# Two MLPs behind an attention block: stages run one by one over all tokens, with a seven-product form in halves of 384 tokens

## The chip, the cores and the metric

The kernel runs on one core of a Trainium2 chip. The metric is the device time of one execution in microseconds (us). Its instructions go to five engines: TensorE (PE, matmuls, with weight loads shown apart as PEld), VectorE (DVE), ScalarE (ACT), GpSimd (POOL) and SyncE (SP, which issues most DMAs).

## The reference

```python
# attention over q, k, v of shape (4, 8, 576, 64), causal, plus a memory term M_prev, z_prev
x = (g * mem_out + (1 - g) * local)            # 2304 tokens x 512
# first MLP, 1536 hidden columns
h = silu(x @ moe_w_gate) * (x @ moe_w_val)     # 2304 x 1536
y = h @ moe_w_out                              # 2304 x 512
# second MLP, 2048 hidden columns
u = y @ moe2_w_in
a = where(u >= 1, u, where(u <= -1, 0, (u + 1)**2 / 4))
out = a @ moe2_w_out                           # 2304 x 512
```

## The kernel before

All matrix products of the MLPs are done with each operand cut in a high and a low part (`PARTS`, line 1067): three matmuls, low by high, high by low and high by high, make one product. A unit `f` is 128 hidden columns, 12 of them in the first MLP and 16 in the second. The MLP weights come in an encoded form and are decoded on chip (`Weights.number`, lines 873 to 941: on DVE two masks, a clamp, a shift, a multiplication and an addition; then `split` makes the two parts).

Two plans are made one after the other by the class `Plan` (line 112), a list scheduler: each task has an engine, a cost, a priority, dependencies and buffers, and the simulated order is the order in which each engine gets its instructions. The engines themselves then run in that order and wait on semaphores.

The first plan is attention, 16 pairs of heads (`Attention.pair`, line 412), four for each batch entry of 576 tokens. Scores, maxima, exponentials, a scaling on POOL (line 735), transposes on PE (lines 769, 786 and 746), copies of these, and the product with the values (`av`, lines 811 and 818). Each pair's result is stored to `xs` in DRAM (line 847). Three groups of 512 tokens (`GROUPS`, line 58) also get their gate and value products for the first six units in this plan (`early_unit`, line 1107, operand tile `xh`, matmuls of line 1074): 432 matmuls of 512 columns, 144 for each group, whose results are stored in DRAM (`gv`).

The second plan is both MLPs. Tokens go in five blocks (`BLOCKS`, line 51: four of 512, one of 256). Block by block: gate and value products (`up_matmuls`, line 1070, operand `xb`), SiLU and product (`hidden`, line 1251), the products with `moe_w_out` (`down`, line 1408), which accumulate over the 12 units in four PSUM banks, and then `pieces` (line 1431), which makes from one block of y the seven operands of a Winograd form of Strassen's scheme and stores them (`ys`). The second MLP runs in three phases of units (`PHASES`), and in each over all blocks: `hidden2` (line 1356) does seven products of 256 columns where the plain form has eight, `hidden1` (line 1337) the plain form for the small block; `down2` (line 1596) adds up the output, and partial sums go to DRAM and back between phases. In `hidden2` the copies c1 (line 1394), c5 and c2 (line 1382) on ACT and the sums v1 and v2 (line 1389) on DVE stand between the products, and PE fills these gaps with queued `down2` products (`fill`, line 1332).

Of the kernel before, what the change touches and what calls it, by code (L numbers as in the profile page):

```python
# [11 lines left out]
U32 = mybir.dt.uint32  # L12
# [16 lines left out]
D1 = 8  # L29
UNITS1 = 12  # L30
# [3 lines left out]
NOACT = 4  # L34
WARM = 8
AHEAD = 30
# [3 lines left out]
OWN = 2  # L40
XB, OP, RAW, HP, TP, WA = 12, 5, 3, 3, 3, 5
SU = 2
UNITS, HALVES = 20, 5
PHASES = (2, 3, 3)
OVER, KEPT = 4, 1

GROUP_AT, X_AT = (-58356.8242, -57686.563, -55609.5288), (21938.2824, -38157.4904, 79878.1715)

FIRST = (0, 8, 1, 2, 9, 3, 4, 10, 5, 6, 11, 7)
BLOCK = 512  # L50
BLOCKS = ((0, 512), (512, 512), (1024, 512), (1792, 512), (1536, 256))
LAST = (8, 9, 10, 11, 0, 1, 2, 3, 4, 5, 6, 7)
ORDERS = ((3, 4, 0, 1, 2), (2, 4, 0, 3, 1), (1, 0, 2, 3, 4))
STAYS = 2
HB = BLOCK // 2
HS = S // 2

GROUPS = (512, 1024, 1536, 1920, 2304)
HT = 512
MASKED = -8.0e9  # L60
# [51 lines left out]
class Plan:  # L112
# [7 lines left out]
    def __init__(self, start=None, over=None, lat=None, slow=None, stay=0, turn=0):  # L120

        self.slow, self.stay, self.turn = slow or {}, stay, turn
        self.over, self.late = over, {**self.LAT, **(lat or {})}
        self.tasks, self.caps, self.taken, self.start = [], {}, {}, start or {}
# [10 lines left out]
    def add(self, eng, dur, prio, fn, deps=(), uses=(), lat=0, behind=None, port=False, form=0):  # L135
# [3 lines left out]
             "lat": lat + self.late[eng], "next": [], "follow": [], "wait": 0, "n": len(self.tasks)}  # L139
# [11 lines left out]
    def dma(self, prio, times, fn, deps=(), uses=(), behind=None):  # L151
# [3 lines left out]
        return self.add("DMA", sum(times), prio, lambda: None, [t], uses)  # L155

    def order(self):
# [29 lines left out]
        while len(out) < len(self.tasks):  # L187
            for eng, heap in ready.items():
                if busy[eng]:
                    continue  # L190
                skipped, found, best = [], None, None
                while heap:
# [9 lines left out]
                    if all(len(free[k]) >= v for k, v in need.items()):  # L202
# [3 lines left out]
                        best = best or t  # L206
                    skipped.append(e)
# [643 lines left out]

class Weights:
# [3 lines left out]
    def __init__(self, ctx, tc, units, dram):  # L856
        self.tc, self.nc, self.first = tc, tc.nc, units
        self.dram = dram
        self.pools = [ctx.enter_context(tc.tile_pool(name="w1", bufs=1))]

    def unit(self, place):
        return self.pools[place.slot >= self.first].tile([P, 2, 512], F32R, name="wu", tag=f"wu{place.slot}")

    def half(self, place):
        return self.pools[1].tile([P, 2, 256], F32R, name="wh", tag=f"wh{place.slot}")

    def begin(self, ctx, plan, bufs, name, reuse):
        pool = lambda tag, n: ctx.enter_context(self.tc.tile_pool(name=f"{tag}_{name}", bufs=n, reuse_waits=reuse))
        self.p = {tag: pool(tag, 1 if tag == "wA" else n) for tag, n in bufs.items()}
# [3 lines left out]
    def number(self, plan, src, prio, s, i_F, places, act=True, behind=None):  # L873
# [3 lines left out]
        i_raw, i_S = plan.inst("raw"), plan.inst("wS")  # L877
        words = lambda x: x.rearrange("p (n t) -> p n t", t=2)

        def load():  # L880
            s["raw"] = self.p["raw"].tile([P, 1024], U32, name="raw", tag="raw")
# [61 lines left out]
    def split(self, plan, prio, t, src, dst, n, uses, act=True):  # L943
# [8 lines left out]
                     t, uses)  # L952
# [3 lines left out]
    def parked(self, plan, tag, prio, t, old, tile, shape):  # L956


        store = plan.dma(prio, [364 * shape[-1] // 128], lambda: self.nc.sync.dma_start(home, f32(tile())), [t], [old])
        home = self.dram.tile(shape, F32, name=f"park{store['n']}")  # L960
        return store, home

    def fetched(self, plan, tag, prio, store, home, put, behind):
        new = plan.inst(tag)
        t = plan.dma(prio, [364 * home.shape[-1] // 128], lambda: self.nc.sync.dma_start(f32(put(new)), home), [store], [new],
                     behind=behind)
        return new, t

    def decode(self, plan, tag, src, prio, act=True, behind=None, park=False):
        i_F, i_w = plan.inst("wA"), plan.inst(tag)  # L970
        s = {"i": i_w}

        def dst():
            if "w" not in s:
                s["w"] = self.unit(i_w)
            return s["w"]

        t = self.number(plan, src, prio, s, i_F, [i_w], act, behind)
        s["t"] = self.split(plan, prio, [t], lambda: f32(s["F"]), dst, 512, [i_F, i_w], act)
        if park:  # L980
            s["park"] = [self.parked(plan, tag, prio, s["t"], i_w, dst, (P, 2, 512))]
        return s

    def back(self, plan, s, tags, prio, behind):


        t = []
        for j, ((store, home), tag) in enumerate(zip(s["park"], tags)):
            def put(place, j=j):
                w = self.half(place) if j == 3 else self.unit(place)  # L990
                if "at" in s:
                    s["w"][j] = w
                else:
                    s["w"] = w
                return w

            i, x = self.fetched(plan, tag, prio, store, home, put, behind)
            behind = plan.last
            t.append(x)
            if "at" in s:  # L1000
                s["i"][j] = i
            else:
                s["i"] = i
        s["t"] = t if "at" in s else t[0]
        s["load"] = behind

    def pair(self, plan, tag, half, srcs, prio, behind=None, park=False):
# [5 lines left out]
        places = [plan.inst(tag) for _ in range(3)] + [plan.inst(half)]  # L1013
# [3 lines left out]
        def dst(j):  # L1017
            if j not in w:
                w[j] = self.half(places[3]) if j == 3 else self.unit(places[j])
            return w[j]  # L1020

        t = [self.number(plan, srcs[0], prio, s[0], i_F[0], [*places, *i_F, *i_C], behind=behind)]
        t.append(self.number(plan, srcs[1], prio, s[1], i_F[1], [], behind=s[0]["load"]))
        lo, up = slice(0, 256), slice(256, 512)
# [13 lines left out]
        for fn, deps, uses in combos:  # L1038
            made.append(plan.add("DVE", e_dve2(256), prio, fn, deps + made[-1:], uses))
        ends = [self.split(plan, prio, [t[0]], lambda: F(0, slice(0, 512)), lambda: dst(0), 512, [i_F[0], places[0]])]  # L1040
        for j in (1, 2):
            ends.append(self.split(plan, prio, [made[-1]], lambda j=j: C(j, slice(0, 512)), lambda j=j: dst(j), 512,
                                   [places[j], i_C[j - 1]]))
        ends.append(self.split(plan, prio, [t[1]], lambda: F(1, up), lambda: dst(3), 256, [i_F[1], places[3]]))

        at_ = ((0, 0), (0, 256), (2, 256), (3, 0), (1, 0), (1, 256), (2, 0))
        park = [self.parked(plan, tag, prio, t, places[j], lambda j=j: dst(j), (P, 2, 256 if j == 3 else 512))
                for j, t in enumerate(ends)] if park else None
# [620 lines left out]
```

## Time and profile before

| | |
|---|---|
| median of 3 runs | 1046.08 us (1045.47 to 1047.13) |
| span of the profiled execution, first to last instruction | 1043.8 us |
| own time of the profiled execution | not given; the median of the runs is 2.3 us above its span |
| PE busy | 1029.0 us (99%) |
| mean granted TensorE clock | 0.998 of 2.4 GHz |

The span is what the profile divides; the time of a run is read here as the span and the 2.3 us that lie around it. PE's busy time is that of pipelined matmuls, so the length of a chain of matmuls is read from the starts of its first and of the next one.

### The profile page before, as it was taken

How to read it: one execution, taken by the hardware profiler on the slowest of the kernel's cores; microseconds unless marked ns; L12 is line 12 of the kernel's file. 1: busy time of each engine (PE TensorE's matmuls, PEld its weight loads, DVE VectorE, ACT ScalarE, POOL GpSimd, SP SyncE). 2: the span in 40 equal slices, each digit the busy share in tenths (PEclk: the TensorE clock that was granted, in tenths of full speed). 3: DMA queues.
4: the chain of work that ended last, by engine and by line, in shares of the span. 5: the costliest groups of instructions: out<-in, count | busy, mean ns of one | idle time of the engine just before them, and what ended most of it. 6: DMA issues, size and time to landing. Idle time of an engine off the chain costs nothing.

```text
span 1043.8 us, 17548 instructions
## 1 busy us (share of the span) xinstructions
PE 1029.0 (99%) x6096; PEld 867.2 (83%) x6096; DVE 674.1 (65%) x1515; ACT 564.6 (54%) x1314; POOL 215.8 (21%) x301
## 2 busy tenths in 40 slices
PE   6999999999999999999999999999999999999998
PEld 5667777778788898888888889999899999899997
DVE  4888888870145688868687767844575767643343
ACT  5987898863222355535353435645564555544443
POOL 7899989992000000000000000000000000000000
PEclk9999999999999999999999999999999999999999
DMA  7776663342785799757777797999689878865422
GB/s 179 190 206 186 177 174 115 99 146 105 248 291 192 251 355 362 239 194 253 271 269 281 257 317 262 356 415 401 214 310 334 307 265 279 273 227 184 161 82 82
DMA packets 172074, 248.12 MB, mean 238 GB/s; under 512 B 72913, under 2 KB 99537, under 8 KB 171985
## 3 DMA queue, kind: packets, MB, share of 16 engines
q1 hardware_dynamic: 170078, 245.64, 69.1%
q10 hardware_dynamic: 1906, 1.35, 0.4%
q8 instruction: 49, 0.80, 0.3%
q14 instruction: 41, 0.33, 0.1%
HBM read 165.15 MB, written 81.79 MB: 237 GB/s over the span
## 4 chain that ended last, share of the span: by engine, by line
PE 96%; POOL 1%; DVE 1%; DMA 1%; ACT 0%; issue 0%; SPq 0%; DVEq 0%; POOLq 0%
PE mm L1074 29%; PE acc L1602 19%; PE mm L1323 18%; PE acc L1418 14%; PE av L818 4%; PE s L646 3%; PE t L769 2%; PE av L811 2%; PE s L680 2%; PE t L786 1%; POOL a L735 1%; PE tq L542 1%; PE tk L531 1%; PE tp L600 1%; PE t L746 1%; DMA kn<-in_q_dram 0%
## 5 line engine op out<-in xcount | busy, mean ns | idle before, releaser
L1602 PE MATMUL acc<-wu,h 128*128 128x512 f32 x864 | 210.3, 391 | 0.0
L1074 PE MATMUL mm<-xb,wu 128*128 128x512 f32 (+1 forms) x1008 | 201.0, 359 | 0.0
L1074 PEld LDWEIGHTS mm<-xb,wu 128*128 128x128 f32 x1008 | 170.0, 189 | 28.3
L1602 PEld LDWEIGHTS acc<-wu,h 128*128 128x128 f32 x864 | 157.4, 188 | 29.3
L1323 PE MATMUL mm<-xb,wu 128*128 128x256 f32 x1188 | 153.9, 283 | 0.0
L1323 PEld LDWEIGHTS mm<-xb,wu 128*128 128x128 f32 x1188 | 150.0, 192 | 3.6 <-ACT mm L1394 0.3
L1418 PE MATMUL acc<-h,wu 128*128 128x512 f32 (+1 forms) x720 | 151.8, 368 | 0.0
L1418 PEld LDWEIGHTS acc<-h,wu 128*128 128x128 f32 x720 | 125.7, 189 | 22.4
L1235 ACT CAST h<-t 128x512 fp32r<-128x512 f32 (+1 forms) x140 | 80.7, 579 | 91.8 <-PE acc L1418 36.4
L1238 DVE TENSOR_TENSOR h<-t,h 128x512 fp32r<-128x512 f32 (+1 forms) x140 | 88.1, 634 | 49.8 <-ACT h L1235 49.1
L1307 ACT ACTIVATE t<-mm,half 128x512 f32<-128x512 f32 (+1 forms) x80 | 51.6, 645 | 116.5 <-PE mm L1323 72.2
L1074 PE MATMUL mm<-xh,wu 128*128 128x512 f32 x432 | 106.6, 401 | 0.0
L1313 DVE SCALAR_TENSOR_TENSOR t<-mm,t 128x512 f32<-128x512 f32 (+1 forms) x80 | 50.8, 635 | 75.0 <-ACT t L1310 74.5
L1122 ACT COPY gvo<-mm 128x512 f32<-128x512 f32 (+1 forms) x80 | 43.2, 543 | 99.9 <-PE mm L1074 90.1
L735 POOL TENSOR_SCALAR a<-a,r,OGP 128x256 f32<-128x256 f32 (+4 forms) x144 | 96.0, 677 | 5.1 <-ACT a L667 3.4
L1074 PEld LDWEIGHTS mm<-xh,wu 128*128 128x128 f32 x432 | 80.0, 188 | 19.1 <-issue 0.9
L667 ACT ACTIVATE a<-a,mn 128x256 f32<-128x256 f32 (+3 forms) x128 | 71.0, 566 | 9.8 <-DVE mn L660 9.6
L890 ACT ACTIVATE wA<-raw 128x512 f32<-128x512 f32 x64 | 43.0, 673 | 34.8 <-DMA raw<-in_moe_w_out_dram 18.4
L449 DVE COPY R<-t 128x512 f32<-128x512 f32 (+1 forms) x48 | 30.0, 640 | 44.9 <-PE t L769 44.8
L660 DVE CUSTOM_DVE_ANT_0 a<-s,mask 128x512 f32<-128x512 f32 (+3 forms) x128 | 55.0, 485 | 5.5 <-PE s L646 5.1
L951 ACT CAST wu<-wA 128x512 fp32r<-128x512 f32 x56 | 34.6, 619 | 30.8 <-DVE wA L920 23.1
L895 DVE TENSOR_SCALAR wA<-wA 128x512 f32<-128x512 f32 x68 | 29.8, 439 | 32.5 <-ACT wA L890 31.3
(133 smaller groups left out, 1413.3 us busy)
## 6 DMA issues: line engine op xcount, KB each, us to landing
xb<-ys SPq DMA_DIRECT2D x69, 512.0 KB, 6.3
park<-wu SPq DMA_DIRECT2D x40, 512.0 KB, 6.6
wu<-park SPq DMA_DIRECT2D x40, 512.0 KB, 8.9
xb<-xs SPq DMA_DIRECT2D x32, 512.0 KB, 7.5
gv<-gv SPq DMA_DIRECT2D x32, 512.0 KB, 9.7
ys<-yo SPq DMA_DIRECT2D x31, 512.0 KB, 5.0
gv<-gvo SPq DMA_DIRECT2D x60, 256.0 KB, 3.8
raw<-in_moe_w_out_dram SPq DMA_DIRECT2D x28, 512.0 KB, 7.1
```

What stands on the lines that cost most here:

```text
L660: nc.vector.tensor_tensor_reduce(a, st[f"s{h}{tag}"][:, at_[c]:at_[c] + kl[c]], self.mask0[:, 512 - kl[c]:512], -0.125, 3.0e38, ALU.add, A ...
L667: nc.scalar.activation(a, a, AF.Exp, bias=mn[:, o:o + 1], scale=-1.0, accum_out=sm[:, o, 0:1])
L735: nc.gpsimd.tensor_scalar(a, a, st["mn"]["r"][:, o:o + 1], self.OGP[:, n, o:o + 1], op0=ALU.mult, op1=ALU.mult)
L1074: nc.tensor.matmul(out, kt_of(unit, pw, kt), x[kt][:, px, cols], start=(kt == 0 and i == 0), stop=(kt == KT - 1 and i == 2))
L1122: nc.scalar.copy(s["o", j], s[j][:, 0:gt])
L1235: nc.scalar.copy(s["h"][:, 0], s["t"])
L1238: nc.vector.tensor_sub(s["h"][:, 1], s["t"], f32(s["h"][:, 0]))
L1307: nc.scalar.activation(mk_t(o), src(), AF.Relu, bias=half, scale=0.5)
L1313: nc.vector.scalar_tensor_tensor(o["t"], src(), 1.0, o["t"], op0=ALU.max, op1=ALU.min)
L1323: nc.tensor.matmul(out, pair["k"](k, pw, j), y["x"][piece][:, px, j], start=first and not (i or j), stop=last and j == 1 and i == 2, skip_ ...
L1418: nc.tensor.matmul(state[m][:, 0:n], l, r, start=(begin and i == 0), stop=(end and i == 2), skip_group_check=True)
L1602: nc.tensor.matmul(state[m], s["h"][:, px, m * P:(m + 1) * P], unit["w"][:, pw], start=(begin and i == 0), stop=(end and i == 2), skip_gro ...
```

## The change

The second plan is written anew, and the first one loses two thirds of its early products.

- Attention: only tokens 0 to 511 keep their early products. For the other two groups the tasks stay in the plan as ghosts, which take their simulated time and buffers but issue nothing. The decoded gate and value weights of the first six units lie in slabs that three units share (`SPOTS`).
- Tokens go in three blocks of 768, each in two halves of HB = 384 tokens, so six groups of 384.
- Gate and value of units 0 to 5 for tokens 512 to 2303 are done in the plain form (`plain`), those of units 6 to 11 in the seven-product form (`chain`), for which the operands are made from x (`x_pieces`). The hidden layer is stored to DRAM (`hs`).
- Then all of `moe_w_out` (`down`), group by group; then all of the second MLP's first product in the seven-product form (`chain`, stored unbounded to `h2s`); then all of its second (`down2`), with the bound taken there. There are no partial sums in DRAM.
- The weights that are used in a later stage are decoded early and parked in DRAM (`parked`). PE's order is fixed by hand; every other task has the latest start that PE's order allows as its priority (`late_starts`).
- The first two pairs of x loads of the second plan are issued on POOL's queue, the next on SP's.

```diff
-BLOCKS = ((0, 512), (512, 512), (1024, 512), (1792, 512), (1536, 256))
-HB = BLOCK // 2
-GROUPS = (512, 1024, 1536, 1920, 2304)
+NK = 3
+NG = 2 * NK
+HB = NT // NG
...
+    def late_starts(self, end):
...
+        for t in reversed(self.tasks):
+            at = t["due"]
+            if at is None:
+                ends = [x["prio"][0] - t["lat"] for x in t["next"]] + [end if t["by"] is None else t["by"]]
+                at = min([min(ends) - t["dur"]] + [x["prio"][0] for x in t["follow"]])
+            t["prio"] = (at, t["n"])
...
             t_x[b] = [at.pair(b, n) for n in range(NP)]
-            for tok in [g for g in groups if (g.stop - 1) // S == b < B - 1]:
+            if b < B - 1:
+                tok, ghost = slice(b * HT, (b + 1) * HT), b > 0
                 stored = [[t_x[e][kt] for e in range(tok.start // S, b + 1)] for kt in range(KT)]
-                xh = load_x(plan, xs, fpool, "xh", tok, X_AT[b], stored)
+                xh, last = early_x(tok, X_AT[b], stored, ghost, last)
                 for f in range(D0):
-                    early_unit(plan, at.ps, f, tok, xh, gpool, GROUP_AT[b], "gvo", bank="bank",
-                               own=b == B - 2 and f >= D0 - OWN)
+                    early_unit(f, xh, GROUP_AT[b], b == B - 2 and f >= D0 - 2, ghost)
...
+    def quarter(kb, r, c, ahead, queue="SP"):
...
+            (nc.gpsimd if queue == "POOL" else nc.sync).dma_start(
+                f32(s["x"]), xs[:, 2 * r:2 * r + 2, :, cols(2 * kb + c)])
...
+    def plain(f, qs, c, span, t_out, kept):
...
+                for kt in range(KT):
+                    for i, (pw, px) in enumerate(PARTS):
+                        nc.tensor.matmul(o[:, 0:n], u["k"](pw, kt), qs[kt // 2, c]["at"](px, kt % 2)[:, span],
+                                         start=(kt == 0 and i == 0), stop=(kt == KT - 1 and i == 2))
...
+    def chain(S, x, kind, ends):
...
+        t1 = prod(0, "a", True, [], [i_e])
+        t5 = prod(4, "d", True, [])
+        c1 = add_act(HB, lambda: nc.scalar.copy(bank(s, "e", i_e)[:, 0:HB], P_("a")), [t1], [i_a, i_e])
+        c5 = add_act(HB, lambda: nc.scalar.copy(s5(), P_("d")), [t5], [i_d, h_s])
+        settle()
+        t6 = prod(5, "a", False, [c1])
+        c2 = add_act(HB, lambda: nc.scalar.copy(u2(), P_("a")), [t6], [i_a, h_u])
+        t2 = prod(1, "e", False, [c1])
+        t3 = prod(2, "d", False, [c5])
+        v1 = add_dve(HB, lambda: nc.vector.tensor_add(u2(), u2(), P_("d")), [c2, t3], [i_d, h_u], by=soon())
+        t7 = prod(6, "a", False, [c2])
+        v2 = add_dve(HB, lambda: nc.vector.tensor_add(s5(), s5(), P_("a")), [t7, c5], [i_a, h_s])
...
+    def down(g):
...
+        for i in range(F1 // 2):
...
+            for m in range(KT):
+                marks.append(pe(e_pe(6, HB), lambda m=m, prod=prod: prod(m), [h["t"]] + [y for u in us for y in u["t"]],
+                                [h["i"], state["i"][m]] + [y for u in us for y in u["i"]]))
...
+    for kb, c, queue, ahead in ((0, 1, "POOL", 0), (1, 0, "POOL", 0), (1, 1, "SP", 0)):
+        for r in range(2):
+            qs[kb][r, c] = quarter(kb, r, c, ahead, queue)
...
+    parks = [wts.parked(plan, out_rows(moe_w_out, f)) for f in range(F1)]
...
+        ends = kept + [plain(f, qs[0], 1, slice(HT - HB, HB), t, []) for f in (2 * i, 2 * i + 1)]
...
+    for i in range(D0 // 2):
+        for kb in (1, 2):
+            for c in range(2):
+                t = flat("h")
+                ends = [plain(f, qs[kb], c, slice(0, HB), t, []) for f in (2 * i, 2 * i + 1)]
...
+    for n, (i, j) in enumerate(todo):
+        for kb in range(NK):
...
+            chain(sets[i, j], xp[kb], ("gate", "val")[j], {"T": silus, "t": None if j == 0 else done, "then": then})
...
+    parks2 = [wts.parked(plan, out_rows(moe2_w_out, f), gate(PARK_AHEAD)) for f in range(F2)]
...
+    for kb in range(NK):
+        yp[kb] = y_pieces(kb)
...
+    for p in range(F2 // 2):
+        for kb in range(NK):
...
+            chain(pairs[p], yp[kb], "up", {"T": T, "then": then})
...
+    for g in range(NG):
+        down2(g)
```

One `prod` of a chain is six matmuls of 384 columns, a chain seven of them. In a chain `settle()` issues t4, the last product of the chain before. A `plain` call is 24 matmuls, a `down` call 144 of 384 columns; `y_pieces` calls `down` for both halves of a block and makes the seven operands of its y; a `down2` call is 144 matmuls of 512 columns.

## Rows read from the trace of the kernel before

**Rows 1.** The page: busy time by engine, and 40 slices of the span.
```profile
PE 1029.0 (99%) x6096; PEld 867.2 (83%) x6096; DVE 674.1 (65%) x1515; ACT 564.6 (54%) x1314; POOL 215.8 (21%) x301
...
PE   6999999999999999999999999999999999999998
...
POOL 7899989992000000000000000000000000000000
```

**Rows 2.** Busy time by stretch, PE's early products (tile xh) alone: stretch, length, busy.
```profile
60.00:234.00 174.00, 38.81 (x144) 1.00 0.54 156
234.00:278.40 44.40, 33.96 (x144) 1.00 0.42 153
278.40:330.00 51.60, 33.86 (x144) 1.00 0.76 252
```

**Rows 3.** Timeline of PE, 234 to 330 us: start, length, instructions.
```profile
234.03 32.31 PE L1074 MATMUL mm<-xh,wu 128*128 128x512 f32 x138
...
270.95 0.76 PE L811 MATMUL av<-P,MZ 128*64 128x320 f32 x4
...
278.45 21.73 PE L1074 MATMUL mm<-xh,wu 128*128 128x512 f32 x92
...
312.15 18.08 PE L1074 MATMUL mm<-xb,wu 128*128 128x512 f32 x79
```

**Rows 4.** Timeline of POOL, its last instructions.
```profile
236.34 1.15 POOL L594 TENSOR_TENSOR p<-p,nrm 128x576 f32<-128x576 f32 x1 [2.96 <-DVE nrm L590]
237.48 5.53 POOL L735 TENSOR_SCALAR a<-a,r,OGP 128x256 f32<-128x256 f32 x9
```

**Rows 5.** Timeline of the end.
```profile
1032.88 6.99 PE L1602 MATMUL acc<-wu,h 128*128 128x512 f32 x30
...
1039.94 1.02 SPq L1587 DMA_DIRECT2D out_dram<-oo  x2
```

**Rows 6.** The chain that ended last, in order of time: start, length, what.
```profile
411.55 5.44 PE acc L1418 x24
...
636.37 5.76 PE mm L1074 x48
```

**Rows 7.** Timeline of PE: the end of a pause near the start.
```profile
18.75 0.66 PE L769 MATMUL t<-ident,a 128*128 128x128 f32 x4 [3.90 <-POOL a L735]
```

**Rows 8.** Stretches of PE behind that pause: length, busy, granted clock.
```profile
20.00:22.00 2.00, 1.37 (x7) 0.50 0.64 141
22.00:24.00 2.00, 2.00 (x11) 0.66 0.74 159
```

**Rows 9.** All engines in a stretch of the MLPs.
```profile
400.00:500.00 100.00, 100.00 (x442) 82.79 (x442) 81.07 (x153) 49.48 (x87) 0.00 (x0) 1.00 0.73 253
```

**Rows 10.** Groups by line and shape: busy us, mean ns | idle before.
```profile
L1323 PEld LDWEIGHTS mm<-xb,wu 128*128 128x128 f32 x1188 | 150.0, 192 | 3.6 <-ACT mm L1394 0.3
L1238 DVE TENSOR_TENSOR h<-t,h 128x512 fp32r<-128x512 f32 x112 | 76.7, 687 | 43.6 <-ACT h L1235 43.2
L901 DVE SCALAR_TENSOR_TENSOR wA<-raw,wA 128x512 uint32<-128x512 uint32 x68 | 48.9, 719 | 0.5
...
L898 DVE TENSOR_SCALAR wA<-wA 128x512 uint32<-128x512 uint32 x68 | 30.6, 450 | 0.7
...
L449 ACT COPY R<-t 128x384 f32<-128x384 f32 x48 | 22.4, 478 | 8.5 <-PE t L786 5.7 <-PE t L769 2.2
...
L1389 DVE TENSOR_TENSOR mm<-u,mm 128x256 f32<-128x256 f32 x32 | 13.7, 428 | 37.7 <-PE mm L1323 37.4 <-ACT yo L1496 0.3
```

**Rows 11.** DMA issues: KB each, median us from issue to landing.
```profile
gv<-gv SPq DMA_DIRECT2D x32, 512.0 KB, 9.7
...
xh<-xs SPq DMA_DIRECT2D x12, 512.0 KB, 6.1
```

More of the change, by code (lines that the diff above doesn't have):

```diff
@@ L27 @@
 D0 = 6
-D1 = 8
-UNITS1 = 12
 FIRST_PAIRS = 3
@@ L982, in decode @@
-        return s
[L984 to L1005, printed above, removed]
@@ L1211, in tile_attention_two_moe @@
-    blocks = [slice(e, e + n) for e, n in BLOCKS]
-    size = lambda tok: tok.stop - tok.start
-    first = [(kind, f) for f in range(D0, D1) for kind in ("gate", "val")]
-    first += [(kind, f) for f in FIRST for kind in ("gate", "val", "wout") if (kind, f) not in ready + first]
-    for i, (kind, f) in enumerate(first):
-        table, w, cut = tables[kind]
-        table[f] = wts.decode(plan, "W", cut(w, f), -20 if i < 2 * (D1 - D0) else 10 * FIRST.index(f) - 10,
-                                act=i >= NOACT)
@@ L1219, in tile_attention_two_moe @@
[L1219 to L1231 removed]
+    plan.cap("X", XS, range(X1))
@@ new lines, in tile_attention_two_moe, with pe @@
+    for tag, n in (("wh", WH), ("T", TP), ("su", SU), ("mm", 8)):
+        plan.cap(tag, n)
+    for n, u in enumerate(first):
+        if n % 3 == 0:
+            held = [Inst("X") for _ in range(2)]
+            for j, i in enumerate(held):
+                i.held, i.slot = True, 2 * (n // 3) + j
+        units[u]["i"] = [held[j] for j in {x[0] for x in SPOTS[n % 3]}]
+        units[u]["t"] = []
+    seq, waiting = [], []
+    clock = [0]
+    def pe(cost, fn, deps, uses):
+        t = plan.add("PE", cost, None, fn, deps, uses, behind=seq[-1:])
+        t["due"] = clock[0]
+        clock[0] += cost
+        seq.append(t)
+        return t
@@ new lines, in gate, with add_act, add_dve, bank @@
+    def gate(ahead, t=None):
+        t = clock[0] if t is None else t
+        past = [x for x in seq[-400:] if x["due"] <= t - ahead]
+        return past[-1:]
+    def add_act(n, fn, deps, uses, **kw):
+        return plan.add("ACT", e_act(n), None, fn, deps, uses, **kw)
+    def add_dve(n, fn, deps, uses, **kw):
+        return plan.add("DVE", e_dve2(n), None, fn, deps, uses, **kw)
+    def bank(s, name, i):
+        if name not in s:
+            s[name] = mm.tile([P, HT], F32, name="mm", tag=f"mm{i.slot}")
+        return s[name]
@@ L1320, in product @@
-    def product(pair, y, k, piece, out, first, last):
-        for j in range(2):
-            for i, (pw, px) in enumerate(PARTS):
-                nc.tensor.matmul(out, pair["k"](k, pw, j), y["x"][piece][:, px, j], start=first and not (i or j),
-                                 stop=last and j == 1 and i == 2, skip_group_check=True)
-    seq, queue = [], []
-    def next_pe(cost, prio, fn, deps, uses):
-        seq.append(plan.add("PE", cost, prio, fn, deps, uses, behind=seq[-1:]))
-        return seq[-1]
@@ L1636, in tile_attention_two_moe, with prod @@
-    fill(len(queue))
+        def prod(k, name, begin, deps, more=()):
+            def f():
+                o = bank(s, name, at_[name])[:, 0:HB]
+                for j in range(2):
+                    for i, (pw, px) in enumerate(PARTS):
+                        nc.tensor.matmul(o, S["k"](k, pw, j), x[k]["at"](px, j), start=begin and not (i or j),
+                                         stop=j == 1 and i == 2, skip_group_check=True)
+            return pe(e_pe(6, HB), f, deps + [S["t"][k], x[k]["t"]], [at_[name], S["i"][k], x[k]["i"], *more])
@@ new lines, in tile_attention_two_moe, with make @@
+    for r in range(2):
+        qs[0][r, 0] = quarter(0, r, 0, 8000)
+    xp = {0: x_pieces(qs[0])}
+    for c in range(2):
+        for r in range(2):
+            qs[2][r, c] = quarter(2, r, c, 8000)
+    sets, kept, wout = {}, {}, []
+    todo = [(i, j) for i in range(D0 // 2, F1 // 2) for j in range(2)]
+    long = 3 * 7 * e_pe(6, HB)
+    start = clock[0] + D0 // 2 * 8 * 2 * e_pe(12, HB)
+    due = {x: start + n * long for n, x in enumerate(todo)}
+    def make(i, j):
+        w = (moe_w_gate, moe_w_val)[j]
+        sets[i, j] = wts.pair(plan, [in_cols(w, f) for f in (2 * i, 2 * i + 1)], gate(SET_AHEAD, due[i, j]), seq[-1:])
```

848 lines of the change are left out of this document (390 added, 458 removed).

## The prediction

> **What bounds the kernel now.** I read the page first: PE is busy for 1029.0 of 1043.8 us, and every slice but the first and the last has 90% or more of it; POOL works in the first ten slices only [rows 1]. So PE's work is the time, but for attention, where POOL could bound as well. Then I asked where PE's early products stand. Of 432 matmuls a third, the first group, runs before 234 us, spread through attention; the other 288 come in two lumps behind it, 144 in 234.0 to 278.4 us and 144 in 278.4 to 330 us [rows 2]. The timeline of PE shows them as two almost unbroken runs, and the MLPs begin at 312.15 us [rows 3]. POOL's last instruction ends at 237.48 + 5.53 = 243.0 us [rows 4]. The reader is to see that attention's other engines are done at 243 us, and that PE owes 288 early products after that point: here PE alone bounds. The MLPs' PE work ends at 1032.88 + 6.99 = 1039.87 us, and 3.9 us of copies and output DMA follow [rows 5]. A matmul of 512 columns takes 5.44/24 = 0.2267 us, one of 256 takes 5.76/48 = 0.120 us [rows 6]; at 2.4 GHz the columns alone are 0.2133 and 0.1067, so each matmul costs its columns and 0.0133 us, whichever its width. One of 384 is then 0.160 + 0.0133 = 0.1733 us; no row has one, and the bounds from the two widths beside it differ by nothing.
>
> **The change, part by part.**
>
> *Early products.* 288 matmuls of 512 columns leave, all of them after 234.03 us: 288 x 0.2267 = 65.3 us. Not all of that is gained, since they cover attention's end. Behind 234.03 us PE has only the last pair's transposes and two `av` blocks, and the transposes wait for POOL's nine scalings, 237.48 to 243.0 us [rows 4], which do not move: what stands ahead of 234 us is the first group, and that stays. The two blocks of `av` take 278.45 - 270.95 = 7.5 us [rows 3]. With about 0.85 us for a hop and the last five transposes (an estimate: four take 0.66 us [rows 7]), PE ends attention at 243.0 + 0.85 + 7.5 = 251.35 us. PE now pauses from 234.0 to about 238 us. Such a pause of 3.90 us near the start [rows 7] was followed by a granted clock of 0.50 and 0.66 in the next two stretches of 2 us [rows 8], which is (0.50 + 0.34) x 2 = 1.7 us of lost work, 1.2 GHz being the lower level. I take it as paid again: 253.0 us. Below, nothing is lost: 251.35.
>
> The Trainium skill's page "TensorE: Matmul & The Clock Gate", section "HAM oscillation — how this bites in real kernels", warns of just this: a pause between bursts of matmuls makes the next burst start at the lower clock. By that rule, the trace agrees (0.50 behind the pause).
>
> *Hand-off.* The first `plain` needs two quarters of x, 768 KB each, issued on POOL's queue, so behind POOL's last scaling at 243.0 us. The trace has no DMA of POOL. The nearest rows are 512 KB in 6.1 us at attention's end and 9.7 us at the slowest [rows 11]. At 6.1 x 1.5 = 9.2 us they land at 252.2, just hidden by `av`; at 9.7 x 1.5 = 14.6 us, and one more for issuing two, at 258.6, which would cost 5.6 us. I take hidden, as the tokens 384 to 767 were stored long before and the DMAs have little else to do there, and keep 258.6 for the range.
>
> *MLPs on PE.* From the code: plain 6 units x 24 = 144 matmuls of 256 columns for tokens 512 to 767, and 4 x 144 = 576 of 384; gate and value chains 18 x 42 = 756; `down` 864; second MLP's chains 24 x 42 = 1008; that is 3204 of 384 columns. `down2` has 864 of 512, as before. Sum: 144 x 0.120 + 3204 x 0.1733 + 864 x 0.2267 = 17.3 + 555.4 + 195.9 = 768.5 us. Before it is 1039.87 - 312.15 = 727.7 us [rows 3, 5], so the MLPs grow by 40.8 us: they take over the 288 products as 144 x 256 and 4 halves, and give back a part by seven products for eight. Counted over everything, it is 47,616 columns and 204 matmuls fewer, 19.8 + 2.7 = 22.6 us of PE.
>
> The same page, section "Back-to-back issue gap", puts a warm matmul at its columns over 2.4 GHz and 2.5 ns. By that the 22.6 us would be 19.8 + 0.5 = 20.4 us; the trace has 13.3 ns [rows 6], so the row is used.
>
> *DVE and ACT under the MLPs.* The tightest stretch is plain and chains together, 17.3 + 99.8 + 131.0 = 248 us of PE. On DVE a decoding is three passes of about 0.70 and three of 0.45 us, 3.45 us [rows 10], and with the low part (0.687) 4.1 us. 12 parked units: 50 us. Six sets of two units, with their sums and splits: 6 x 11.3 = 68 us. A pass over 384 columns lies between 0.428 (256) and 0.687 (512), so 0.557; over 768 it is 0.95. Three blocks of x operands, 12 passes of 0.95 each: 34 us. 18 chains with v1 and v2 and nine with four multiplications: 40 us; the plain products' multiplications: 21 us. Together 213 us, 86%. That is near what DVE had in 400 to 500 us, 81 of 100 us with PE at 100 [rows 9], so it stays cover, not bound. ACT has less. The stores and loads of `hs` and `h2s` replace the `ys`, `gv` and partial-sum traffic, and a group's hidden layer is stored two chains, 14.6 us, or more before it is loaded again, against 9.7 us for the slowest load [rows 11].
>
> *Inside a chain.* t6 waits for c1, which waits for t1; t5 and the former chain's t4 stand between, 2 x 6 x 0.1733 = 2.08 us. c1 takes 0.478 us [rows 10] and two hops between engines; one foreign instruction ahead of it on ACT fits in. Before, this turn had six matmuls of 512 columns as cover, 1.36 us, and cost nearly nothing: weight loads of the second MLP waited 3.6 us in all, 0.3 of that for c1 [rows 10]. So the stalls within the MLPs are taken as 4 us, twice the 2.0 us by which the old MLPs (727.7) exceed their matmuls (2160 of 512 and 1968 of 256 columns, 725.8). The bounds are 0 and what the second rival below gives. Stage borders (weights and operands for the next stage share slots with the last one's) are in the 4 us.
>
> *Sum.* 253.0 + 768.5 + 4 + 3.9 = 1029.4 us of span, against 1043.8; with the 2.3 us around it 1031.7, say 1032 us, 1.3% faster.
>
> **Rivals.**
>
> *Attention's end and the borders are dearer.* Quarters land at 258.6 (+5.6), the clock falls once more in that pause (+1.7), and each of the three other stage borders costs 2 to 3 us: 1041 to 1048. For it: no row shows a DMA from POOL, and PE has no filler at any border. Against it: the loads have 8 us of cover.
>
> The page "DMA: Bandwidth & Descriptors", section "SWDGE vs HWDGE vs iDMA", says that POOL's DMAs have descriptors written by software, which DVE can lock out. No row here shows it, and it would only make the landing later.
>
> *Chains wait.* Slower than before: c1, c2 and v2 each stand in a queue that also decodes, and PE has no queued filler in a chain. If a chain loses 0.5 us on its 7.3, 42 chains lose 21 us: 1053. It decides from (1046.1 - 1031.7)/42 = 0.34 us per chain. For it: DVE at 86%; v2 (0.557 us and hops) may find a 0.95 us pass ahead of it, and 2.08 us then just do. Against it: the small waits of before with less cover.
>
> *Attention does not get shorter.* The ghosts keep the order, so if something other than the early products held the `av` blocks at 270.95, the MLPs start at 278.45 and the time is about 1057. Against it: POOL is done at 243.0, and the runs of early products stand right ahead.
>
> *POOL moves up.* Fewer loads and copies pull the last scalings forward, nothing pauses: 1020 to 1026.
>
> **How the numbers follow.** Forecast (1024 to 1042) 0.66; dearer borders 0.14, of which 0.09 still faster and 0.05 the same; chains wait 0.12, slower; attention not shorter 0.03, slower; POOL moves up 0.05, faster. Faster by over 0.2%, which is about what a measurement of this kernel can tell from no change: 0.80; within it 0.05; slower 0.15. The range 1024 to 1050 leaves out about 2 in 10: the fastest case, the worst of the chains and the third rival.
>
> **What would show it.** Right: the first matmul of the MLPs at 251 to 254 us with xh at 144 matmuls; 384-column matmuls at 0.173 us in unbroken runs; PE's work from there to its end 768 to 775 us; DVE about 85% busy up to 500 us. Wrong: pauses of PE that recur with every chain, waiting for ACT or DVE; a long pause ahead of the first `plain`; a run of 384 columns at more than 0.175 us a matmul; `av` still at 270 us.

## The result and the profile after

The kernel with the change takes 1030.78 us (1029.82 to 1032.01), the one before 1046.36 us (1045.47 to 1047.13) on the same chip: a ratio of 0.9856, interval 0.9842 to 0.9870. The span of the profiled execution is 1028.0 us against 1043.8, its own time 1029.82.

The page, busy time by engine and the slices of PE and POOL, answers to [rows 1]:

```profile
PE 1004.1 (98%) x5892; PEld 907.8 (88%) x5892; DVE 705.9 (69%) x1483; ACT 576.5 (56%) x1247; POOL 219.9 (21%) x309
...
PE   6999999996999999999999999999999999999998
...
POOL 7899889994000000000000000000000000000000
```

PE has 24.9 us less to do and is idle 9.1 us more (1028.0 - 1004.1 against 1043.8 - 1029.0). The new hole is the 6 in the tenth slice. PE's timeline around it (start, length, instructions; in brackets the idle time before and its releaser), beside [rows 3]:

```profile
233.91 0.27 PE L745 MATMUL t<-ident,a 128*128 128x128 f32 x1
242.16 3.05 PE L766 MATMUL t<-ident,a 128*128 128x128 f32 x14 [7.98 <-POOL a L732]
...
246.88 0.76 PE L808 MATMUL av<-P,MZ 128*64 128x320 f32 x4
...
254.39 45.80 PE L1353 MATMUL mm<-xw 128*128 128x256 f32 x307
```

POOL's last instructions, beside [rows 4]:

```profile
237.38 5.52 POOL L732 TENSOR_SCALAR a<-a,r,OGP 128x256 f32<-128x256 f32 x9
242.85 3.20 POOL L1275 DMA_DIRECT2D xw<-xs  x4
```

POOL did not move. PE stands still until the eighth of the nine scalings, then does all 30 remaining transposes in 4.7 us, then the two `av` blocks in 7.5 us, and the MLPs begin at 254.39 us with no pause. Stretches of PE there (stretch, length, busy of PE, PEld, DVE, ACT, POOL, granted clock, DMA), beside [rows 8]:

```profile
238.00:242.00 4.00, 0.00 (x0) 0.00 (x0) 0.18 (x1) 0.00 (x0) 4.00 (x7) 0.51 0.00 0
242.00:244.00 2.00, 1.84 (x9) 1.85 (x10) 0.26 (x1) 0.48 (x1) 2.00 (x4) 0.50 0.00 0
244.00:246.00 2.00, 2.00 (x16) 2.00 (x15) 1.64 (x3) 0.43 (x1) 2.00 (x3) 0.78 0.70 145
246.00:248.00 2.00, 2.00 (x17) 1.34 (x17) 0.69 (x1) 1.72 (x8) 0.05 (x1) 1.00 1.00 384
```

The clock was at its lower level, 1.2 GHz, when the transposes began, and that cost (0.50 + 0.22) x 2 = 1.4 us. So much for attention's end. From there the chain that ended last, in order of time, shows the second MLP, beside [rows 5, 6]:

```profile
653.36 173.68 PE mm L1402 x1002
...
832.22 191.82 PE mm L1534 x846
1024.04 0.02 issue
```

1002 matmuls of 384 columns in 173.68 us are 0.1733 us each, the predicted price to the last digit, and the run is unbroken. PE's work in the MLPs lasts from 254.39 to 1024.04 us, 769.65 us. Groups by line and shape (busy, mean ns, idle before), beside [rows 10]:

```profile
L1402 PE MATMUL mm<-xw 128*128 128x384 f32 x1512 | 269.8, 335 | 0.5 <-DVE xw L951 0.5
...
L1480 PE MATMUL mm<-xw 128*128 128x384 f32 x864 | 150.1, 334 | 0.0
L1353 PE MATMUL mm<-xw 128*128 128x384 f32 x576 | 100.0, 334 | 0.0
```

In all MLP stages PE waited once, 0.5 us. (The mean of one matmul overlaps the next one; a run's length is divided by its count instead.) DVE in the stages with plain products and chains, beside [rows 9]:

```profile
254.40:371.80 117.40, 117.40 (x724) 117.40 (x723) 88.25 (x152) 40.64 (x74) 0.00 (x0) 1.00 0.68 238
371.80:502.60 130.80, 130.30 (x752) 129.98 (x752) 104.74 (x215) 68.39 (x141) 0.00 (x0) 1.00 0.44 151
```

The x loads by queue (KB each, median us to landing), beside [rows 11]:

```profile
xw<-xs SPq DMA_DIRECT2D x8, 768.0 KB, 12.2
...
xw<-xs POOLq DMA_DIRECT2D x4, 768.0 KB, 7.4
```

### The profile page after: what moved, and what is told of

It is laid out like the page before. It is cut to its first block, busy times and chain, and to the rows that moved or that the text cites. A ratio compares the mean times of both kernels' runs of the same rounds, so it can differ in the third digit from the quotient of the medians.

```text
span 1028.0 us, 16598 instructions
## 1 busy us (share of the span) xinstructions
PE 1004.1 (98%) x5892; PEld 907.8 (88%) x5892; DVE 705.9 (69%) x1483; ACT 576.5 (56%) x1247; POOL 219.9 (21%) x309
## 4 chain that ended last, share of the span: by engine, by line
PE 94%; POOL 3%; DMA 1%; DVE 1%; issue 1%; SPq 0%; POOLq 0%; DVEq 0%
PE mm L1402 30%; PE mm L1534 19%; PE mm L1480 15%; PE mm L1353 11%; PE av L815 4%; PE mm L1166 3%; PE s L643 3%; PE t L766 2%; PE av L808 2%; POOL a L732 1%; PE s L677 1%; PE t L783 1%; PE tq L539 1%; PE tp L597 1%; PE tk L528 1%; PE t L743 1%
## 5 line engine op out<-in xcount | busy, mean ns | idle before, releaser
L1402 PE MATMUL mm<-xw 128*128 128x384 f32 x1512 | 269.8, 335 | 0.5 <-DVE xw L951 0.5
L1402 PEld LDWEIGHTS mm<-xw 128*128 128x128 f32 x1512 | 262.7, 188 | 0.9 <-DVE xw L951 0.8
L1534 PE MATMUL mm<-xw 128*128 128x512 f32 x864 | 196.2, 390 | 0.0
L1534 PEld LDWEIGHTS mm<-xw 128*128 128x128 f32 x864 | 162.3, 188 | 33.5
L1480 PE MATMUL mm<-xw 128*128 128x384 f32 x864 | 150.1, 334 | 0.0
L1480 PEld LDWEIGHTS mm<-xw 128*128 128x128 f32 x864 | 149.8, 188 | 0.0
L1353 PE MATMUL mm<-xw 128*128 128x384 f32 (+1 forms) x720 | 117.4, 324 | 0.0
L1353 PEld LDWEIGHTS mm<-xw 128*128 128x128 f32 x720 | 117.1, 189 | 0.2 <-issue 0.2
L1523 DVE SCALAR_TENSOR_TENSOR t<-r,t 128x768 f32<-128x768 f32 x48 | 46.0, 958 | 39.2 <-ACT t L1522 37.6
L1297 DVE TENSOR_TENSOR xw<-t,xw 128x768 fp32r<-128x768 f32 x48 | 46.0, 957 | 37.0 <-ACT xw L1294 37.0
L888 ACT ACTIVATE wA<-raw 128x512 f32<-128x512 f32 x68 | 45.6, 677 | 21.3 <-DMA raw<-in_moe_w_out_dram 15.7
L1424 ACT COPY mm<-mm 128x384 f32<-128x384 f32 x42 | 19.5, 465 | 57.5 <-PE mm L1402 57.5
L1402 PE MATMUL mm<-xw,wh 128*128 128x384 f32 x252 | 50.4, 334 | 0.0
L1520 ACT ACTIVATE t<-r,half 128x768 f32<-128x768 f32 x48 | 44.9, 936 | 8.9 <-DMA r<-h2s 8.0
L815 PE MATMUL av<-R,vn 128*64 128x320 f32 (+4 forms) x448 | 48.7, 357 | 0.0
L899 DVE SCALAR_TENSOR_TENSOR wA<-raw,wA 128x512 uint32<-128x512 uint32 x68 | 48.3, 716 | 0.3
```

The costliest lines, as they stand in the source:

```text
L815: nc.tensor.matmul(o[rg][halves[h], c0:c1], st["vn"][:, kc, h], r, start=False, stop=i == len(terms[rg]) - 1, tile_position=(0, h * 64), s ...
L899: nc.vector.scalar_tensor_tensor(s["F"], words(s["raw"])[:, :, 1], 0xC0000000, s["F"], op0=ALU.bitwise_and, op1=ALU.bitwise_or)
L1297: nc.vector.tensor_sub(s["x"][:, :, 1], t(), f32(s["x"][:, :, 0]))
L1353: nc.tensor.matmul(o[:, 0:n], u["k"](pw, kt), qs[kt // 2, c]["at"](px, kt % 2)[:, span], start=(kt == 0 and i == 0), stop=(kt == KT - 1 an ...
L1402: nc.tensor.matmul(o, S["k"](k, pw, j), x[k]["at"](px, j), start=begin and not (i or j), stop=j == 1 and i == 2, skip_group_check=True)
L1480: nc.tensor.matmul(o, u["k"](pw, m), h["at"](px, j), start=(i == 0 and j == 0 and n == 0), stop=(i == F1 // 2 - 1 and j == 1 and n == 2), ...
```

## The experiments

Three theories needed telling apart. The first is the prediction's: PE's work sets the time one for one, but for a few us at attention's end. Against it: the gain comes from something else that the new second plan does; or it is larger on PE and partly lost in waits that errors of opposite sign hide.

**All early products run again, two thirds of their results unused.**

```diff
-                tok, ghost = slice(b * HT, (b + 1) * HT), b > 0
+                tok, ghost = slice(b * HT, (b + 1) * HT), False
...
+                xh["kept"] = b == 0
...
-                    if not ghost:
+                    if x["kept"]:
                         nc.sync.dma_start(gv[f // 2][j][:, f % 2], s["o", j])
```

> All 288 early products of tokens 512 to 1535 run in attention again, and their results are dropped (the MLPs compute them as in the changed kernel). Theory (they stand on PE's path behind 234 us): the MLPs begin near 312 us as before, 57.8 us later than in the changed kernel, whose time of 1030.8 becomes 1086 to 1090 us. Rival (attention's end is held by something else, and the products were mostly cover): less than 1045 us.

Measured: 1088.28 us, one run. PE's timeline is that of before [rows 3]:

```profile
234.54 32.31 PE L1166 MATMUL mm<-xh,xw 128*128 128x512 f32 x138
...
271.45 0.76 PE L808 MATMUL av<-P,MZ 128*64 128x320 f32 x4
...
278.96 33.87 PE L1166 MATMUL mm<-xh,xw 128*128 128x512 f32 x144
312.66 7.58 PE L1354 MATMUL mm<-xw 128*128 128x256 f32 x62
```

So what held `av` back to 271 us were the early products, and the third rival falls. 57.5 us more than the change, against 65.3 us of added matmuls: the other 7.8 had covered attention's end.

**The kernel before, with that move alone.** Early products of tokens from 512 on are done at the MLPs' start, in the old order and form.

```diff
-            for tok in [g for g in groups if (g.stop - 1) // S == b < B - 1]:
+            for tok in [g for g in groups if (g.stop - 1) // S == b < 1]:
...
-        for f in [f for f in range(D1) if tok in late or f >= D0]:
+        for f in [f for f in range(D1) if tok.start or f >= D0]:
```

> The kernel before with one part of the change alone: the early products of tokens from 512 on leave attention and are done at the start of the MLPs, in the old form. Theory: PE's work stays, attention's end loses its cover as in the changed kernel (a pause of 8.0 us and some at the lower clock), so 7 to 10 us slower than before, 1053 to 1056 us, with the first matmul of the MLPs near 254 us. Rival (the products only filled time that something else would fill): within 2 us of before.

Measured: 1055.57 us, ratio 1.0090 (1.0073 to 1.0107): 9.5 us slower than before (1046.06 us, measured beside it). PE after attention:

```profile
248.06 0.96 PE L1074 MATMUL mm<-xb,wu 128*128 128x512 f32 x3
254.50 65.71 PE L1074 MATMUL mm<-xb,wu 128*128 128x512 f32 x356 [5.48 <-DMA xb<-xs]
```

Attention ends 6 us earlier than in the changed kernel, and PE then waits 5.48 us for x. The expectation had the time right but not the place: it counted on the pause of 8.0 us. This plan has no ghosts, so PE does one pair's `av` during POOL's scalings; it loses its time in the wait for x and at the granted clock behind it (0.50 from 254 to 258 us, 0.76 to 262). The move by itself is a loss: the same matmuls, and a bare end of attention. So the gain is that of the fewer matmuls in the new form. The prediction counted 22.6 us of them; less the 7.8 us of lost cover of the run above it is 14.8 us, and 15.6 were measured. The changed kernel without ghosts, further below (1029.79 us), does attention's end in the same order as this run, and is 25.8 us faster: 22.6 us of matmuls, 2.0 us less waiting for x (3.5 against 5.5), and 1.2 us not assigned.

**One more product in every chain.** Product 1 is summed twice, 252 matmuls of 384 columns more.

```diff
-                for j in range(2):
+                for j in (0, 1, 0, 1) if k == 1 else (0, 1):
```

> In each of the 42 chains the second product is done twice, six more matmuls of 384 columns (the output has that product twice). Theory (PE is the bound within the chains, and what the seven-product form saves is PE time one for one): 252 x 0.1733 = 43.7 us more, 1074 to 1076 us. Rival (DVE or ACT bounds the chains): under 1055 us.

Measured: 1074.18 us, one run: 43.4 us for 252 matmuls, 0.172 us each, against 0.1733 us by rows. Time follows PE's work one for one in the chains. The Trainium skill's page "TensorE: Matmul & The Clock Gate", section "Back-to-back issue gap", has columns over 2.4 GHz and 2.5 ns for an isolated matmul, 41.0 us here as an estimate; the run and the unbroken rows above are nearer to the columns and 13 ns.

**Slack of a chain.** c1 is copied four times instead of once, 1.40 us more of ACT in each of 42 chains.

```diff
-        c1 = add_act(HB, lambda: nc.scalar.copy(bank(s, "e", i_e)[:, 0:HB], P_("a")), [t1], [i_a, i_e])
+        c1 = add_act(HB, lambda: [nc.scalar.copy(bank(s, "e", i_e)[:, 0:HB], P_("a")) for _ in range(4)], [t1], [i_a, i_e])
```

> The copy c1 of every chain is done four times over, 1.40 us more on ACT between t1 and t6 (same result). From the rows of the changed kernel c1 takes 0.465 us, and two products, 2.08 us, stand in for it. Theory (the turn has some 1.2 us to spare, so the second rival was far off): 42 chains lose 0.2 to 0.5 us each, 1039 to 1052 us. Rival (the turn is already tight, each us of ACT shows in full): 42 x 1.40 = 59 us, 1085 us and more. A second (ACT has more room than that): the same as the changed kernel.

Measured: 1044.52 us, ratio 0.9987 (0.9977 to 0.9997), 13.7 us over the change. PE's weight loads by wait (us in total, times, longest):

```profile
PEld mm L1402 <- ACT mm L1424: 14.9, 41, 1.4
```

Now c1 delays 41 of 42 chains, by 0.33 us a chain. So 1.40 - 0.33 = 1.07 us of the 2.08 us of cover was free. The second rival's mechanism is a real one, for c1 at least, but its point of decision lies 1.4 us of ACT away. Its other link, v2 on DVE, was never what PE waited for, so its slack is not shown.

**The first x loads on SP's queue instead of POOL's.**

```diff
-    for kb, c, queue, ahead in ((0, 1, "POOL", 0), (1, 0, "POOL", 0), (1, 1, "SP", 0)):
+    for kb, c, queue, ahead in ((0, 1, "SP", 0), (1, 0, "SP", 0), (1, 1, "SP", 0)):
```

> The first two pairs of x loads go on SP's queue in place of POOL's. Theory: on POOL they are issued at 242.9 us and hidden under av; on SP they stand behind the last store of attention, issued at 255.4 us, and take 7.4 us and more to land, so the MLPs begin 8 to 12 us later: 1038 to 1043 us. Rival (loads are fast enough or wait for buffers anyway): within 2 us of the changed kernel.

Measured: 1042.06 us, ratio 0.9963 (0.9950 to 0.9977), 11.3 us over the change. SP's and PE's timelines, and a stretch of PE:

```profile
254.43 4.03 SPq L844 DMA_DIRECT2D xs<-x  x2
258.51 1.57 SPq L1275 DMA_DIRECT2D xw<-xs  x2
```

```profile
264.70 1.62 PE L1353 MATMUL mm<-xw 128*128 128x256 f32 x6 [7.50 <-DMA xw<-xs]
267.02 53.21 PE L1353 MATMUL mm<-xw 128*128 128x256 f32 x334 [0.71 <-DMA xw<-xs]
```

```profile
265.00:268.00 3.00, 2.29 (x10) 2.00 (x10) 0.54 (x1) 0.54 (x1) 0.00 (x0) 0.50 1.12 346
268.00:275.00 7.00, 7.00 (x44) 7.00 (x43) 2.30 (x5) 2.42 (x6) 0.00 (x0) 0.68 1.08 362
```

On SP the loads stand behind the stores of attention's last outputs and go out at 258.51 us, 15.7 us later than on POOL. The span of this execution is 14.0 us longer (it was one of the longer ones of its kernel): 8.2 us of waits, 0.50 x 2.3 + 0.32 x 7 = 3.4 us at a reduced clock, and 2.7 us by which this attention ended later. This is the first rival's mechanism, as far as it concerns the loads and the clock, and POOL's free queue is what kept it away. The transfer itself is not faster there: on SP the two loads landed 6.0 us after their issue.

**Ghosts taken out of the plan.** PE's order then no longer counts on work that is not issued.

```diff
-            if b < B - 1:
+            if b < 1:
```

> The ghosts leave the plan of attention, so that the simulated order knows that PE is free at the end; same work as in the changed kernel. Theory (the pause is as long as it is since the order puts on PE's queue first the transposes of a late one of POOL's nine scalings): the transposes follow POOL, av ends near 248 to 251 us, and the loads of x (issued at 242.9, 7.4 us to land) are next: MLPs from 251 us, 1026 to 1029 us. Rival (POOL's scalings alone set the end): the same as the changed kernel, 1030 to 1032 us.

Measured: 1029.79 us, ratio 0.9843 (0.9828 to 0.9858), which overlaps the interval of the change: not told apart. PE waits for POOL's scalings 5.7 instead of 12.9 us in all, and the first MLP matmul comes at 249.86 us, 5.4 us after POOL's last scaling instead of 11.5; then:

```profile
249.86 0.94 PE L1353 MATMUL mm<-xw 128*128 128x256 f32 x6 [0.61 <-DMA xw<-xs]
253.71 66.50 PE L1353 MATMUL mm<-xw 128*128 128x256 f32 x416 [2.90 <-DMA xw<-xs]
```

What the transposes gain, the x loads take. They are issued behind POOL's scalings, as in the changed kernel, and POOL ended later here:

```profile
238.92 5.53 POOL L732 TENSOR_SCALAR a<-a,r,OGP 128x256 f32<-128x256 f32 x9
244.40 3.20 POOL L1275 DMA_DIRECT2D xw<-xs  x4
```

The expectation was 1026 to 1029 us, and the run came out above it.

**Early products back into the pause.** Gate and value of units 0 and 1 for tokens 512 to 767 return to attention, 48 matmuls of 256 columns (5.8 us), and leave the plain stage; the buffers for them are widened by 256 tokens.

```diff
-                tok, ghost = slice(b * HT, (b + 1) * HT), b > 0
+                tok, ghost = slice(b * HT, (b + 1) * HT), b > 1
+                if b == 1:
+                    tok = slice(HT, HT + 256)
...
-                    early_unit(f, xh, GROUP_AT[b], b == B - 2 and f >= D0 - 2, ghost)
+                    early_unit(f, xh, GROUP_AT[b], b == B - 2 and f >= D0 - 2, ghost or b == 1 and f >= 2, tok)
...
-        ends = kept + [plain(f, qs[0], 1, slice(HT - HB, HB), t, []) for f in (2 * i, 2 * i + 1)]
+        ends = kept if 2 * i < 2 else kept + [plain(f, qs[0], 1, slice(HT - HB, HB), t, []) for f in (2 * i, 2 * i + 1)]
```

> The gate and value products of units 0 and 1 for tokens 512 to 767 (48 matmuls of 256 columns, 5.76 us) go back from the MLPs to attention, where the changed kernel pauses for 8.0 us ahead of its last transposes. Theory (attention's end is the only place with free PE time): the MLPs begin no later, a pause of 2 us is left, the lower clock behind it (1.3 us) mostly goes, and the MLPs lose 5.8 us: 1023 to 1026 us. Rival (attention's end waits for something that the products hold up, a bank or ACT): 1030 us or more.

Measured: 1025.46 us, ratio 0.9802 (0.9787 to 0.9817). PE:

```profile
234.03 6.19 PE L1166 MATMUL mm<-xh,xw 128*128 128x256 f32 x48
242.67 2.18 PE L766 MATMUL t<-ident,a 128*128 128x128 f32 x18 [2.45 <-POOL a L732]
```

The pause shrinks from 7.98 to 2.45 us, the granted clock stays at 1.00, and 5.3 us come back, about the 5.8 us of moved work. This version beats both kernels by more than the intervals.

**The same with four units, and with six.** They take 96 and 144 matmuls back. With four:

```diff
-                    early_unit(f, xh, GROUP_AT[b], b == B - 2 and f >= D0 - 2, ghost or b == 1 and f >= 2, tok)
+                    early_unit(f, xh, GROUP_AT[b], b == B - 2 and f >= D0 - 2, ghost or b == 1 and f >= 4, tok)
...
-        ends = kept if 2 * i < 2 else kept + [plain(f, qs[0], 1, slice(HT - HB, HB), t, []) for f in (2 * i, 2 * i + 1)]
+        ends = kept if 2 * i < 4 else kept + [plain(f, qs[0], 1, slice(HT - HB, HB), t, []) for f in (2 * i, 2 * i + 1)]
```

> The same for units 0 to 3: 96 matmuls, 11.5 us, more than the pause of 8.0 us. Theory: all of the pause and the lower clock go, the rest only moves: 8.0 + 1.3 us less than the changed kernel, 1020 to 1023 us. Rival (the products beyond the pause hold up the transposes and copies behind them): no better than with two units, 1024 us or more.

> The same for units 0 to 5: 144 matmuls, 17.3 us, 9.3 more than the pause. Theory: PE's time only moves, so the same as with four units, 1020 to 1024 us. Rival (what stands behind the pause is held up): slower than with four units by 2 us or more.

Measured: 1044.99 us, ratio 0.9983 (0.9974 to 0.9993), and 1055.03 us, ratio 1.0086 (1.0070 to 1.0101). Both ranges of the theory were missed, by over 20 us. The times are those of the rivals, but the rivals put the loss right behind the pause, and most of it stands elsewhere. PE by wait, with four units:

```profile
PE mm L1482 <- DMA xw<-park: 19.0, 4, 9.5
```

The waits stand in the stage `down`, 260 us behind the edit: PE wants decoded `moe_w_out` before it has been parked and read back. Between these waits the granted clock is lower, 0.67 from 520 to 545 us. With six units PE waits 16.7 us for parked weights. That run is slower still for what stands near the pause: PE waits 2.3 us for ACT's copies of the early products among the last transposes and 5.3 us in the first plain products, and the granted clock is 0.93 from 254 to 300 us. What leads to the waits in `down` shows in SP's timeline, in the raw loads of `moe_w_out` (start, length, count). With four units:

```profile
262.66 11.11 SPq L1277 DMA_DIRECT2D xw<-xs  x8
273.82 3.51 SPq L883 DMA_DIRECT2D raw<-in_moe_w_out_dram  x3
```

In the changed kernel:

```profile
258.71 1.15 SPq L1275 DMA_DIRECT2D xw<-xs  x2
259.96 1.74 SPq L883 DMA_DIRECT2D raw<-in_moe_w_out_dram  x3
...
262.55 11.68 SPq L1275 DMA_DIRECT2D xw<-xs  x6
```

With the shorter plain stage SP issues all eight x loads ahead of the raw loads (a load's priority is its latest start), which go out 13.9 us later. The decoding then lacks its input: from 274 to 285 us DVE is busy for 1.11 us, against 8.96 in the changed kernel. By 351 us SP has issued four raw loads of `moe_w_out` and four units are parked, instead of nine and nine. The twelfth unit is stored (start, length, count) with four units at

```profile
525.48 0.43 SPq L987 DMA_DIRECT2D park<-pk  x1
```

and in the changed kernel at

```profile
484.58 0.33 SPq L987 DMA_DIRECT2D park<-pk  x1
```

That is 32 us behind the first matmul of `down` (493.80 us) in the one, and 18 us ahead of it (502.56 us) in the other.

**Four units, and half of the decoding.** Only six of the twelve units of `moe_w_out` are decoded and parked, and each is used for two; the decoding of the other six is left out.

```diff
-    parks = [wts.parked(plan, out_rows(moe_w_out, f)) for f in range(F1)]
+    parks = [wts.parked(plan, out_rows(moe_w_out, f)) for f in range(F1 // 2)] * 2
```

> As e_fill4, which stalled 19 us for parked weights in the down stage, but only six of the twelve units of moe_w_out are decoded and parked, and each is used twice (the first MLP's second product has the wrong weights for half its units). Theory (DVE's decoding, 4.1 us a unit, came too late once the plain stage was 11.5 us shorter and its loads stood behind eight x loads): the stall goes, 1020 to 1024 us. Rival (the loads of parked weights themselves, or their buffers, are late): 1035 us or more.

Measured: 1021.49 us, ratio 0.9762 (0.9746 to 0.9779), and no wait for parked weights. So the loss hangs on the decoding, its loads and stores with it, being late, and filling with four units is worth 9.3 us where it is not.

**Four units, the first three raw loads ahead of the x loads.**

```diff
+    for p in parks[0:3]:
+        p["load"]["due"] = -1.0e5
```

> As e_fill4, but SP issues the loads of the first three encoded units of moe_w_out ahead of the x loads, at about 258 us in place of 274 us, so that DVE can decode in the first 40 us of the MLPs; all twelve units are decoded. Theory (late decoding): three units more are parked by 350 us, seven against four, and the stall of 19 us shrinks to 0 to 10: 1022 to 1034 us; if the loss is in full at the five units that are missing, the upper end. Rival (something else in the down stage): 1043 us or more.

Measured: 1036.92 us, ratio 0.9909 (0.9894 to 0.9924), just over the expected range. Waits for parked weights fall from 19.0 to 6.7 us, but the x loads behind the three now cost 3.8 us and with them some clock (0.93 from 254 to 300 us). SP's order is part of the cause; this run doesn't show it to be all of it.

**Four units, the raw loads between the x loads, two steps of each decoding on POOL.**

```diff
+    for p in parks[0:3]:
+        p["load"]["due"] = 1.0e4
...
-        t = self.number(plan, src, None, s, i_F, [i_F], behind=behind, i_raw=i_w)
-        t = self.split(plan, None, [t], lambda: f32(s["F"]), dst, 512, [i_F, i_w])
+        t = self.number(plan, src, None, s, i_F, [i_F], behind=behind, i_raw=i_w, pool=True)
+        t = self.split(plan, None, [t], lambda: f32(s["F"]), dst, 512, [i_F, i_w], pool=True)
```

> As the kernel that takes units 0 to 3 back into attention's pause (1045.0 us, with 19.0 us of PE waits for parked weights), with two edits to the parking of moe_w_out: the last addition of the decoding and the subtraction for the low part go from VectorE to GpSimd for the twelve parked units, and the raw loads of the first three are due at 10 us of the plan, between the x loads instead of behind them. If VectorE's late decoding is what the down stage waits for, the parks are stored earlier, the wait for them falls to a few us and the time is 1021 to 1028 us, from 1021.5 of the run with half the decoding upwards. If what is late is the raw buffers and SyncE's order of loads, or if GpSimd and VectorE hold each other up, the waits for parked weights stay above 8 us and the time is 1030 to 1046 us.

Measured: 1035.00 us, ratio 0.9905 (0.9889 to 0.9922): on the side of the second theory by its time, though the waits for parked weights themselves fell below its 8 us. By wait:

```profile
PE mm L1405 <- ACT mm L1427: 5.1, 1, 5.1
...
PE mm L1483 <- DMA xw<-park: 3.9, 1, 3.9
```

From 254 to 545 us ACT waits for raw loads less (5.1 us, against 24.8 with four units), but now for POOL, whose addition takes 1736 ns in the mean from 509 to 560 us, where DVE's takes 0.69 us in the run with four units. Groups of POOL there, and one such wait in ACT's timeline:

```profile
L918 POOL TENSOR_TENSOR wA<-wA,wS 128x512 f32<-128x512 f32 x6 | 10.4, 1736 | 32.1 <-DVE wS L907 32.1
```

```profile
652.83 0.62 ACT L950 CAST pk<-wA 128x512 fp32r<-128x512 f32 x1 [3.32 <-POOL wA L918]
```

The wait ends 4 us ahead of the point (656.91 us) where PE has waited 5.1 us for ACT's first c1 of the second MLP; that the one causes the other was not tested. Part of the stall moved instead of going: the two waits are 9.0 of the 13.5 us to the run with half the decoding, and behind them the granted clock is lower (0.94 from 520 to 545 us, 0.98 from 653 to 830). Which share of the lateness is SP's order and which the raw buffers (a parked result lies in the buffer of a raw load until it is stored) stays open.

## Why the prediction was right

**The size.** Forecast 1032 us, measured 1030.78. By terms, on the span: the MLPs' start 254.4 us against 253.0 (+1.4); PE's matmuls and stalls 769.65 against 768.5 + 4 (-2.9); the tail 4.0 against 3.9 (+0.1). The sum is 1028.0 against 1029.4. Two errors of opposite sign made the agreement closer than the steps were. Around the span lie 1.8 us (1029.82 against 1028.0), where 2.3 were taken.

**Early products** were right: 144 matmuls of `xh` stay, the rest are gone, and the run that puts them back has `av` at 271.45 us. **Attention's end** was mis-sized. The prediction had a pause to "about 238 us", and after POOL's last scaling 0.85 us of transposes and 1.7 us of lost clock. The pause lasted to 242.16 us: PE's order, which still counts the ghosts, has the transposes of the eighth scaling's result ahead of those that were ready. From POOL's end, 242.9 us, to `av` it took 4.0 us where 2.55 were allowed, 1.4 of them clock. The price of 1.7 us was also read too coarsely. [rows 8] leave out the first stretch behind the pause of 3.90 us, from 18.75 to 20 us, where the granted clock was still 0.98; so that burst did not start at the lower clock, though the prediction says so. Priced by PE's busy time, what followed cost 0.50 x 1.37 + 0.34 x 2 = 1.4 us. The Trainium skill's page "TensorE: Matmul & The Clock Gate", section "HAM oscillation — how this bites in real kernels", says that a pause makes the next burst begin at the lower clock. By that rule, the trace agrees for the changed kernel, with 0.50 behind the 7.98 us pause, and again 0.50 behind the 7.50 us of x loads on SP.

**The hand-off** was right: POOL's loads landed in 7.4 us where 9.2 were taken, and `av` hid them. The run with SP's queue shows what it would have cost else, 11.3 us: the first rival (1041 to 1048) is a real case in its first two terms, one queue away; its third, 2 to 3 us at each other border, did not show, since no wait there was over 0.5 us. On POOL's descriptors, of which the Trainium skill's page "DMA: Bandwidth & Descriptors" warns in "SWDGE vs HWDGE vs iDMA", no delay shows here; DVE was busy only 3.35 us of the 10 us from 244 to 254, so the rule is not put to the test.

**Matmuls of 384 columns** were right to four digits, by the 13.3 ns that [rows 6] gave at the two widths beside it. **Stalls** were 1.2 us, not 4; the doubling was too careful: no border between stages cost more than the one wait of 0.5 us. **DVE** had 193 of 248 us, 78%, not 213. The passes were counted rightly, but added up wrongly: their lengths in the trace sum to 214.9 us, and they overlap. A pass over 768 columns that starts at 299.21 us lasts 0.95 us, and the next one starts at 300.08. The 81 of 100 us that the sum was compared with is busy time, without that overlap. **The chains'** cover was rightly called enough: for c1 1.07 us of it is left.

What the prediction did not see is what lies next to it. It asked whether DVE is busy enough to be the bound, and 78% says no. It did not ask when each decoding gets its input: there the new plan has little room. A kernel 5.8 us shorter ahead of `down` still meets it with 0.7 us of wait, one 11.5 us shorter loses 19.0 us.

## What to carry to other kernels

Where one engine is busy 99% of the time, count its instructions, price each from an unbroken run and divide a run's length by its count; the rest is the seams, and a seam costs what the next engine is late, and the slower clock behind the pause. Before you shorten a stage, ask which work of other engines was hidden under it for a later stage, and when that work gets its input; a mean busy share does not show it. When you add up an engine's passes, mind that their lengths can overlap, and compare busy time with busy time. Fill a pause with work that some later stage gives up, in small steps, and time each step.

## What was not expected of the hardware

- The overhead of a matmul with its weight load was the same 13.3 ns at three widths (0.120, 0.1733 and 0.2267 us for 256, 384 and 512 columns).
- A 768 KB load issued on POOL's queue took 0.8 us of POOL (3.20 us for four) and landed in 7.4 us (9.2 in the run without ghosts). On SP's queue the same kind of load took 12.2 us in a busier stretch, and 6.0 us for the first two in the run with SP's queue: what the change of queue gained was the earlier issue.
- POOL's addition of 128x512 numbers took 1.74 us in the mean of six, and 1.3 to 2.9 us in the 40 of that run, where DVE's took 0.69 us.
- Instructions of DVE that follow each other overlap in the trace, by about 0.08 us where one starts right behind the other, so the sum of their lengths (214.9 us) exceeds the engine's busy time (193.0).
